# Expert stage of a fused attention, gated-layer and expert kernel: additions, scatters and gathers moved to later steps of the next unit

## The chip, the core and the metric

The kernel runs on one core of one Trainium2 chip. A time is microseconds on the device for one execution. Engines are named as the profile names them: PE (TensorE, matrix multiplication; PEld its weight loads), DVE (VectorE), ACT (ScalarE), POOL (GpSimd), SP (SyncE, which issues most DMAs). Each engine works through its own list of instructions in order. An instruction that waits holds up everything behind it on its engine. The clock of TensorE is granted by a throttle, and the profile shows the granted share.

## The reference

Three layers follow one another; the change lies in the last.

```python
def reference(**kwargs):
    attn_out = _attn_ref(**attn_kwargs)                 # queries pooled by 2, 16 heads of 64
    x = attn_out ... reshape(B * S, H * D)              # 1152 tokens of 512
    x = _moe_ref(x=x, **moe_kwargs)                     # rms norm, silu(x @ w_gate) * (x @ w_val) @ w_out
    return _moe2_ref(x=x, **moe2_kwargs)

def _moe2_ref(x, w_gate, w_noise, noise, w1, w2):
    ...                                                 # noisy logits of 8 experts, two best per token
    out = np.zeros((N, D), dtype=np.float32)
    for e in range(E):
        for k in range(2):
            mask = top2[:, k] == e
            if not mask.any():
                continue
            h = np.maximum(x[mask] @ w1[e], 0.0)        # 512 -> 1024
            out[mask] += top2_w[mask, k, None] * (h @ w2[e])   # 1024 -> 512
    return out.astype(np.float32)
```

All data are float32. A product on PE is made of three passes over operands that are split into a rounded part and a remainder ("hi" and "lo").

## The kernel before, in words

The tokens of an expert are put into blocks of 128. The expert stage, from about 537 us to the end, works through 14 **units** (`SEQ`, with two units ahead of it that the first half of the router chose). A unit is a **pair** (two blocks of one expert) or a **single** (one block). In the kernel before the units are pair, pair, pair, single, pair, single, pair, single, pair, single, pair, single, pair, pair, numbered 0 to 13. A further set of units stands in a branch that is taken only when there are more blocks; it isn't taken with these inputs.

Each unit has eight **steps** (0 to 7), one per piece of 512 KB of that expert's weights (`W[u, i]`, split into hi by ACT, L106, and lo by DVE, L1005, five steps ahead by `wsplit`). Steps 0 to 3 are the first layer (`up_pair` L1072 or `up_one` L1087). In a pair each step ends with `up_evac`: ACT makes the rounded hidden part (L1076), DVE the remainder (L1077). The PSUM tile `ph` has two buffers, so step 2 waits for the evacuation of step 0, and step 3 for that of step 1. In a single the hidden rows are evacuated by ACT and turned on PE by `h_trans`, half 0 after step 2 and half 1 after step 4. Steps 4 to 7 are the second layer (`down`, L1099), which adds up into a PSUM tile `py` for each block.

Around them run, in program order:

- `finish(u)`: for each block DVE computes `yo = py * weight + pr` (L1131; L1129 in unit 0, which adds nothing), and POOL issues the scatter of the rows to the output (L1132). The next scatter waits for the one before to land, because both write the output. Before, the call for unit u stands after step 0 of unit u + 1.
- `gather_o(u)`: POOL issues the gather of the output rows that unit u will add to (tile `pr`, L1027), one per block. It waits until the scatters of unit u - 1 have landed. Before, it stands after step 2 of unit u.
- `gather_x(u + 2)` (tile `xg`, L1021) after step 5 of unit u: input rows for the unit after the next, also on POOL; its buffer comes free when `x_trans(u + 1)` and `weight(u + 1)` (DVE, `wv`), at the same step, have read it.
- `x_trans` and `h_trans` go through `tsplit`: four transposes on PE, the rounded part by ACT (L975), the remainder by DVE (L977). They share two PSUM banks in turn (`bank()`), so in a single the four calls h 0, h 1, x block 0, x block 1 alternate between the banks. The transposes of x block 1 wait until DVE has evacuated h 1.

The last unit, 13, is followed by its own `finish`, block 0 and then block 1, after all its `down` steps, which alternate between the blocks.

Unit 0 is written out by hand at the end of the program, interleaved with the second half of the router. There `run(gB)` issues the rest of `r_assign`: positions of the tokens (`pp`), sums on POOL (`sm`, `mx`, L747 and L749), a count per expert on PE (`pn`, L754), and a row of small DVE operations. The PSUM pool of units 1 to 13 (`pm`, opened by `open_psum`) lies over the banks of the earlier pool. Its tiles get their places in the order in which their names are first used: before, `ph` first and then `py`.

Of the kernel before, what the change touches and what calls it, by code (L numbers as in the profile page):

```python
# [9 lines left out]
F32 = mybir.dt.float32  # L10
# [11 lines left out]
def fused_kernel(ctx, tc, q, k, v, w_gate, w_val, w_out, rms_g,  # L22
                 r_gate, r_noise, noise, e_w1, e_w2, out, dbg=None):
    nc = tc.nc
    P = 128
# [482 lines left out]
    DM = H * D  # L508
# [132 lines left out]
    def bank_(spec, nm):  # L641
        pl, tg, nb = spec
        return pl.tile([P, 512], F32, name=nm, tag=tg, bufs=nb)
# [79 lines left out]
    def r_assign(t0, nt):  # L723
        ts_ = slice(t0, t0 + nt)
        M, mmb = R["M"], R["mmb"]
        idx = R["idx"][:, ts_]
        n = nt * NE
        pp = bank_((ps, "gv1", 2) if t0 else BANK[0], "pp")[:, 0:n].rearrange("p (t e) -> p t e", t=nt)
        for t in range(t0):
            pe.matmul(pp, R["onesb"], mmb[:, t, None, :].to_broadcast([P, nt, NE]), start=(t == 0), stop=False)  # L730
        dve.tensor_copy(idx, R["x8"][:, ts_, 0:2])
        yield
        dve.tensor_tensor(M[:, ts_], R["i8"][:, None, None, :].to_broadcast([P, nt, 2, NE]),
                          idx[:, :, :, None].to_broadcast([P, nt, 2, NE]), op=ALU.is_equal)
        yield
        dve.tensor_tensor(mmb[:, ts_], M[:, ts_, 0], M[:, ts_, 1], op=ALU.add)
        yield 1
        pe.matmul(pp, R["lt"], mmb[:, ts_], start=(t0 == 0), stop=False)
        for t in range(nt - 1):
            pe.matmul(pp[:, t + 1:], R["onesb"], mmb[:, t0 + t, None, :].to_broadcast([P, nt - 1 - t, NE]),  # L740
                      start=False, stop=(t == nt - 2))
        P_ = R["S"][:, 0, ts_]
        mx, sm = rtile(f"mx{t0}", [P, NE, NT], BF16), rtile(f"sm{t0}", [P, nt, NE], BF16)
        with nc.allow_low_precision("integers up to 5"):
            a = mmb[:, t0]
            for t in range(1, nt - 1):
                pool.tensor_tensor(sm[:, t], a, mmb[:, t0 + t], op=ALU.add)  # L747
                a = sm[:, t]
            pool.tensor_tensor(mx, a[:, :, None].to_broadcast([P, NE, NT]),  # L749
                               mmb[:, t0 + nt - 1, :, None].to_broadcast([P, NE, NT]), op=ALU.add)  # L750
        if t0:
            PB["n"] = bank_((ps, "gv1", 2), "pn")
            for m in ("mx0", f"mx{t0}"):
                pe.matmul(PB["n"][0:NCOL, 0:2], R[m].rearrange("p e j -> p (e j)"), R["onesb"][:, 0:2],  # L754
                          start=(m == "mx0"), stop=(m != "mx0"))
        dve.tensor_tensor(P_, pp, R["base8"][:, None, :].to_broadcast([P, nt, NE]), op=ALU.add)
        yield
        dve.tensor_tensor(M[:, ts_], M[:, ts_], P_[:, :, None, :].to_broadcast([P, nt, 2, NE]), op=ALU.mult)
        yield
        aki, cs = R["aki"][:, :, ts_], R["cs"][:, :, ts_]  # L760
        with nc.allow_low_precision("integers below 2 ** 24"):
            dve.tensor_reduce(aki[:, 0], M[:, ts_], axis=AX.X, op=ALU.add)
        yield
        dve.tensor_scalar(aki[:, 1], aki[:, 0], 7, None, op0=ALU.logical_shift_right)
        yield
        dve.tensor_scalar(aki[:, 2], aki[:, 0], 127, None, op0=ALU.bitwise_and)
        yield
        dve.tensor_copy(cs, aki[:, 1:3])
        yield
# [147 lines left out]
    def r_index(pl):  # L917
# [12 lines left out]
    RAW = []  # L930
    REG = {}
    SEQ = [None, None] + [(True, 0), (False, 0), (True, 1), (False, 1), (True, 2), (False, 2), (True, 3), (False, 3),
                          (True, 4), (False, 4), (True, 5), (True, 6)]
    NU1 = len(SEQ)
    SEQ += [(True, r) for r in range(NPS, NPA)] + [(False, r) for r in range(NSS, NSA)]

    def nblk(u):
        return 2 if u < 2 or SEQ[u][0] else 1
# [48 lines left out]
    def experts():  # L987
        mo = ctx.enter_context(tc.tile_pool(name="mo", bufs=1, reuse_waits="tile"))
# [35 lines left out]
        def gather_o(u):  # L1024
            PR[u] = wps[0].tile([P, 2, DM], F32, name="pr", tag="ws21", bufs=1)
            for k in range(nblk(u)):
                pool.indirect_dma_start(out=PR[u][:, k], out_offset=None, in_=out,  # L1027
                                        in_offset=bass.IndirectOffsetOnAxis(ap=col(u, k, "gidx"), axis=0))
# [61 lines left out]
                act.activation(HS[u, h], PL[u, h], AF.Relu)  # L1090

        def down(u, i, k):
            if i == 4:
                PL[u, "y", k] = pbank("py")
            w, x = W[u, i], HTT[u]
            f0 = 2 * (i - 4)
            for z, (a, c) in enumerate(PASS):
                for d in range(2):
                    pe.matmul(PL[u, "y", k], x[c][:, f0 + d, k * P:k * P + P], w[a][:, d],  # L1099
                              start=i == 4 and z + d == 0, stop=i == 7 and z == 2 and d == 1)  # L1100

        def piece(u, i):
            if i >= 4:
                for k in range(nblk(u)):
                    down(u, i, k)
            elif nblk(u) == 2:
                up_pair(u, i, 0)
                up_pair(u, i, 1)
                up_evac(u, i)
            else:  # L1110
                up_one(u, i)
# [8 lines left out]
                                         op0=ALU.is_equal, op1=ALU.mult)  # L1120
            dve.tensor_tensor(wv[:, 2, 0:n], wv[:, 0, 0:n], wv[:, 1, 0:n], op=ALU.add)

        def finish(u):
            n = nblk(u)
            yo = YO[u] = mo.tile([P, 2, DM], F32, name="yo", tag="yo", bufs=1)
            for k in range(n):
                w = WV[u][:, 2, k:k + 1]
                if u == 0:
                    dve.tensor_scalar(yo[:, k], PL[u, "y", k], w, 1.0, op0=ALU.mult, op1=ALU.mult)  # L1129
                else:  # L1130
                    dve.scalar_tensor_tensor(yo[:, k], PL[u, "y", k], w, PR[u][:, k], op0=ALU.mult, op1=ALU.add)  # L1131
                pool.indirect_dma_start(out=out, out_offset=bass.IndirectOffsetOnAxis(ap=col(u, k, "sidx"), axis=0),  # L1132
                                        in_=yo[:, k], in_offset=None, bounds_check=B * SQ - 1, oob_is_err=False)
# [7 lines left out]
        def units(u0, u1, skip=0):  # L1141
            todo = [(u, i) for u in range(u0, u1) for i in range(8)]
            if not skip:
                gather_x(u0)
                gather_o(u0)
                for i in range(8):
                    wload(u0, i)
                for a in todo[:LEAD]:
                    wsplit(*a)
                x_trans(u0)  # L1150
                weight(u0)
                if u0 + 1 < u1:
                    gather_x(u0 + 1)
                    for i in range(8):
                        wload(u0 + 1, i)
                for u, i in todo[:LEAD]:
                    if u + 2 < u1:
                        wload(u + 2, i)
            for n_, (u, i) in enumerate(todo):
                if n_ < skip:  # L1160
                    continue
                piece(u, i)
                if nblk(u) == 1:
                    if i == 2:
                        h_trans(u, 0)
                    if i == 4:
                        h_trans(u, 1)
                if i == 0 and u > max(u0, 1):
                    finish(u - 1)
                if i == 2 and u > max(u0, 1):  # L1170
                    gather_o(u)
                if i == 5 and u + 1 < u1:
                    x_trans(u + 1)
                    weight(u + 1)
                    if u + 2 < u1:
                        gather_x(u + 2)
                if n_ + LEAD < len(todo):
                    v_, j = todo[n_ + LEAD]
                    wsplit(v_, j)
                    if v_ + 2 < u1:  # L1180
                        wload(v_ + 2, j)
            finish(u1 - 1)

        def open_psum():
            pm.append(ctx.enter_context(tc.tile_pool(name="pm", bufs=1, space=PSUM, reuse_waits="tile")))

        def rest():
            open_psum()
            units(0, NU1, 8)
            more = nc.values_load(R["more"][0:1, 0:1], min_val=0, max_val=1)  # L1190
            with tc.If(more > 0):
                units(NU1, len(SEQ))
# [53 lines left out]
    for f in range(2, NFP - 2):  # L1246
        u0 = 32 * f
# [17 lines left out]
    def run(g, n=1000):  # L1265
        if n < 1000 and skip.get(id(g), 0):
            skip[id(g)] -= 1
            return
        for z in itertools.islice(g, n):
            if z and n < 1000:  # L1270
                skip[id(g)] = z - 1
                return
# [111 lines left out]
    run(gB, 1)  # L1384
    up_evac(0, 3)
    down(0, 4, 0)
    run(gB)
    w_hi(0, 7)
    down(0, 4, 1)
    run(gW)  # L1390
    run(gC, 2)
    x_trans(1)
# [61 lines left out]
```

## Time and profile before

| | |
|---|---|
| median of 3 runs | 847.99 us (843.16 to 853.68) |
| profiled execution | 845.21 us, span of its instructions 843.3 us |
| busy in the span | PE 791.6 us, DVE 580.2 us, ACT 421.4 us, POOL 299.7 us |
| mean granted clock of PE | 0.979 |

A row of a timeline reads: start in us, duration, engine, line, operation, destination and sources, shape, and in brackets how long the engine sat idle before it and what released it. A row of waits reads: engine and line that waited, for whom, us in total, how many times, and the longest.

### The profile page before, as it was taken

How to read it: one execution, taken by the hardware profiler on the slowest of the kernel's cores; microseconds unless marked ns; L12 is line 12 of the kernel's file. 1: busy time of each engine (PE TensorE's matmuls, PEld its weight loads, DVE VectorE, ACT ScalarE, POOL GpSimd, SP SyncE). 2: the span in 40 equal slices, each digit the busy share in tenths (PEclk: the TensorE clock that was granted, in tenths of full speed). 3: DMA queues.
4: the chain of work that ended last, by engine and by line, in shares of the span. 5: the costliest groups of instructions: out<-in, count | busy, mean ns of one | idle time of the engine just before them, and what ended most of it. 6: DMA issues, size and time to landing. Idle time of an engine off the chain costs nothing.

```text
span 843.3 us, 14036 instructions
## 1 busy us (share of the span) xinstructions
PE 791.6 (94%) x5282; PEld 681.8 (81%) x5282; DVE 580.2 (69%) x838; ACT 421.4 (50%) x823; POOL 299.7 (36%) x251
## 2 busy tenths in 40 slices
PE   5999999999897989999999999989998999999993
PEld 4777777767675779999999999879987988888992
DVE  6668668677678866766787646686684876777750
ACT  4655655656565644442333252554464646456530
POOL 8747647649233521311132100112232432323410
PEclk9999999999999989999999999999999999999997
DMA  7344222221132211422141016639997888888210
GB/s 208 87 135 146 66 90 71 73 69 30 43 115 72 80 51 51 147 78 76 54 147 54 1 52 230 204 127 367 320 308 249 283 273 290 254 277 293 98 47 21
DMA packets 72940, 118.83 MB, mean 141 GB/s; under 512 B 7583, under 2 KB 37279, under 8 KB 72865
## 3 DMA queue, kind: packets, MB, share of 16 engines
q1 hardware_dynamic: 67504, 101.55, 38.0%
q0 software_dynamic: 5360, 16.31, 5.6%
q8 instruction: 43, 0.70, 0.4%
q14 instruction: 33, 0.26, 0.1%
HBM read 103.66 MB, written 10.77 MB: 136 GB/s over the span
## 4 chain that ended last, share of the span: by engine, by line
PE 67%; DVE 12%; issue 7%; DMA 4%; ACT 4%; POOL 4%; POOLq 0%; DVEq 0%; ACTq 0%
PE gv L528 14%; PE py L1099 11%; PE ph L1072 8%; PE po L549 8%; PE av L229 7%; PE st L202 4%; PE s L188 3%; DMA pr<-out_dram,gidx 3%; PE st L203 3%; PE ph L1087 3%; PE tt L135 2%; DVE wz L1005 2%; DVE Ql L193 1%; PE xt L972 1%; DVE es L217 1%
## 5 line engine op out<-in xcount | busy, mean ns | idle before, releaser
L528 PE MATMUL gv<-XN,ws 128*128 128x256 f32 (+1 forms) x1152 | 168.2, 299 | 4.1 <-ACT sl L536 3.7
L528 PEld LDWEIGHTS gv<-XN,ws 128*128 128x128 f32 x1152 | 159.8, 191 | 10.1 <-ACT sl L536 3.9
L1005 DVE TENSOR_TENSOR wz<-raw,wz 128x1024 fp32r<-128x1024 f32 x112 | 133.9, 1221 | 16.5 <-ACT wz L106 16.2
L193 DVE TENSOR_REDUCE Ql<-s 128x1 fp32r<-128x1152 f32 x72 | 97.3, 1354 | 57.5 <-PE s L188 43.5
L1099 PE MATMUL py<-wz,hTT 128*128 128x512 f32 x552 | 134.2, 395 | 0.0
L204 ACT ACTIVATE et<-st 128x288 f32<-128x288 f32 x288 | 103.0, 413 | 52.5 <-PE st L203 48.2
L106 ACT CAST wz<-raw 128x1024 fp32r<-128x1024 f32 x112 | 113.4, 1046 | 8.0 <-PE py L1099 8.0
L1099 PEld LDWEIGHTS py<-wz,hTT 128*128 128x128 f32 x552 | 100.7, 188 | 20.3 <-DVE hTT L977 0.9
L1072 PE MATMUL ph<-xgT,wz 128*128 128x256 f32 x768 | 95.3, 285 | 9.0 <-DVE hTT L1077 7.7
L1072 PEld LDWEIGHTS ph<-xgT,wz 128*128 128x128 f32 x768 | 94.1, 191 | 10.8 <-DVE hTT L1077 8.4
L398 POOL TENSOR_TENSOR ws<-wm,ws 128x1024 fp32r<-128x1024 f32 x18 | 43.3, 2407 | 151.1 <-ACT ws L397 97.0
L202 PE MATMUL st<-QH,KT 128*128 128x288 f32 x288 | 91.1, 331 | 5.5 <-ACT et L204 4.0
L549 PE MATMUL po<-ws,hT 128*128 128x512 f32 x324 | 84.5, 400 | 0.1
L203 PE MATMUL st<-QlT,KT 128*128 128x288 f32 x288 | 81.9, 298 | 0.0
L229 PE MATMUL av<-et,v 128*64 128x288 f32 x576 | 81.5, 419 | 0.0
L202 PEld LDWEIGHTS st<-QH,KT 128*128 128x128 f32 x288 | 55.0, 191 | 20.4 <-ACT et L204 11.7
L549 PEld LDWEIGHTS po<-ws,hT 128*128 128x128 f32 x324 | 59.5, 192 | 11.1 <-ACT hT L538 0.5
L217 POOL TENSOR_TENSOR accp<-accp,et 128x576 f32<-128x576 f32 x32 | 48.2, 1507 | 55.7 <-ACT et L204 35.1
L1132 POOL DMA_INDIRECT out_dram<-yo,sidx x23 | 29.2, 1271 | 103.2 <-DVE yo L1131 51.3
L538 ACT CAST hT<-sl 128x256 fp32r<-128x256 f32 (+1 forms) x48 | 20.8, 433 | 88.8 <-DVE sl L537 88.8
L229 PEld LDWEIGHTS av<-et,v 128*64 128x64 f32 x576 | 37.6, 138 | 26.0 <-issue 5.9
L1076 ACT ACTIVATE hTT<-ph 128x512 fp32r<-128x512 f32 x36 | 21.6, 599 | 70.3 <-PE ph L1072 70.3
(250 smaller groups left out, 1172.8 us busy)
## 6 DMA issues: line engine op xcount, KB each, us to landing
raw<-in_moe_w_dram SPq DMA_DIRECT2D x112, 512.0 KB, 5.7
wraw<-in_moe_w_gate_dram SPq DMA_DIRECT2D x6, 1024.0 KB, 5.1
wraw<-in_moe_w_val_dram SPq DMA_DIRECT2D x6, 1024.0 KB, 7.9
wraw<-in_moe_w_out_dram SPq DMA_DIRECT2D x6, 1024.0 KB, 5.3
kraw<-in_k_dram SPq DMA_DIRECT2D x16, 288.0 KB, 4.1
v<-in_v_dram SPq DMA_DIRECT2D x8, 576.0 KB, 3.7
KT<-KT SPq DMA_DIRECT2D x16, 288.0 KB, 3.2
Qraw<-in_q_dram SPq DMA_DIRECT2D x16, 256.0 KB, 4.5
```

The costliest lines, as they stand in the source:

```text
L106: act.copy(o, i)
L193: dve.tensor_reduce(Ql[p % 3][h][:, c, D:D + 1], t[:, :, 0:384], axis=AX.XY, op=ALU.max, negate=True)
L202: pe.matmul(t[:, 0:NG], KT[p, h][:, cs], QhT[p, h][:, n0:n0 + NG], start=True, stop=False)
L203: pe.matmul(t[:, 0:NG], KT2[h][p % NKT[h]][:, cs], QlT[p, h][:, n0:n0 + NG], start=False, stop=True)
L204: act.activation(et[:, h, :], t[:, 0:NG], AF.Exp, scale=SCALE)
L217: eng.tensor_tensor(acc, acc, e, op=ALU.add)
L229: pe.matmul(av[h * D:(h + 1) * D, 0:NG], V[p][:, h, c, :], ET[p, g, c][:, h, :], start=(c == 0), stop=(c == KC - 1))
L528: pe.matmul(t[:, 0:n], w[a][:, d, j * P:(j + 1) * P], XN[hf][b_][:, d, cs], start=(k_ == 0), stop=(k_ == 11))
L549: pe.matmul(pt, HT[f, hf][a][:, j, c0:c0 + P], w[b_][:, j, :], start=(k_ == 0), stop=(k_ == 5))
L1005: eng.tensor_tensor(lo, RAW[u % 2][i], hi.bitcast(F32), op=ALU.subtract)
L1072: pe.matmul(o, w[a][:, d, j * P:j * P + P], XT[u][c][:, d], start=z + d == 0, stop=z == 2 and d == 3)
L1099: pe.matmul(PL[u, "y", k], x[c][:, f0 + d, k * P:k * P + P], w[a][:, d], start=i == 4 and z + d == 0, stop=i == 7 and z == 2 and d == 1)
```

## The change

Five edits. (1) `finish(u - 1)` is called after step 3 of unit u, no longer after step 0, and `gather_o(u)` after step 6, no longer after step 2, so behind `gather_x(u + 2)`. In the last unit both are called after step 1. (2) Units 11 and 12 change places: the order is now pair (10), pair (11), single (12), pair (13). (3) In the last unit the second layer is done block by block: the four `down` steps of block 0, its `finish`, then those of block 1. (4) `py` is the first tile that the PSUM pool gives out, so it lies on the banks where `ph` lay before, and `ph` on later banks. (5) The count per expert (`pn`) is issued one `down` later in unit 0.

```diff
         if t0:
+            yield
             PB["n"] = bank_((ps, "gv1", 2), "pn")
...
-                          (True, 4), (False, 4), (True, 5), (True, 6)]
+                          (True, 4), (True, 5), (False, 4), (True, 6)]
...
-            if i == 4:
+            if (u, "y", k) not in PL:
                 PL[u, "y", k] = pbank("py")
...
-        def finish(u):
-            n = nblk(u)
-            yo = YO[u] = mo.tile([P, 2, DM], F32, name="yo", tag="yo", bufs=1)
-            for k in range(n):
+        def finish(u, ks=None):
+            if u not in YO:
+                YO[u] = mo.tile([P, 2, DM], F32, name="yo", tag="yo", bufs=1)
+            yo = YO[u]
+            for k in range(nblk(u)) if ks is None else ks:
...
-                piece(u, i)
+                last = u == u1 - 1
+                if not last or i < 4:
+                    piece(u, i)
                 if nblk(u) == 1:
                     if i == 2:
                         h_trans(u, 0)
-                    if i == 4:
+                    if i == 4 - last:
                         h_trans(u, 1)
-                if i == 0 and u > max(u0, 1):
-                    finish(u - 1)
-                if i == 2 and u > max(u0, 1):
-                    gather_o(u)
+                if u > max(u0, 1):
+                    if i == (1 if last else 3):
+                        finish(u - 1)
+                    if i == (1 if last else 6):
+                        gather_o(u)
...
-            finish(u1 - 1)
+
+            u = u1 - 1
+            for k in range(nblk(u)):
+                for i in range(4, 8):
+                    down(u, i, k)
+                finish(u, [k])
...
             open_psum()
+            PL[1, "y", 0] = pbank("py")
             units(0, NU1, 8)
...
-    run(gB)
+    run(gB, 1)
     w_hi(0, 7)
     down(0, 4, 1)
+    run(gB)
```

On DVE, in unit 3 (a single), before. `hTT` are the remainders of the hidden rows, halves 0 and 1; `xgT` that of the next unit's input:

```order
569 L1131 SCALAR_TENSOR_TENSOR yo<-py,wv,pr 128x512 x2
570 L1005 TENSOR_TENSOR wz<-raw_5869,wz 128x1024
571 L1005 TENSOR_TENSOR wz<-raw_5870,wz 128x1024
572 L977 TENSOR_TENSOR hTT<-xt,hTT 128x4x128
573 L1005 TENSOR_TENSOR wz<-raw_5871,wz 128x1024
574 L1005 TENSOR_TENSOR wz<-raw_5581,wz 128x1024
575 L977 TENSOR_TENSOR hTT<-xt,hTT 128x4x128
576 L1005 TENSOR_TENSOR wz<-raw_5581,wz 128x1024
577 L977 TENSOR_TENSOR xgT<-xt,xgT 128x4x128 x2
```

and in the changed kernel:

```order
569 L1006 TENSOR_TENSOR wz<-raw_5869,wz 128x1024
570 L1006 TENSOR_TENSOR wz<-raw_5870,wz 128x1024
571 L978 TENSOR_TENSOR hTT<-xt,hTT 128x4x128
572 L1006 TENSOR_TENSOR wz<-raw_5871,wz 128x1024
573 L1133 SCALAR_TENSOR_TENSOR yo<-py,wv,pr 128x512 x2
574 L1006 TENSOR_TENSOR wz<-raw_5581,wz 128x1024
575 L978 TENSOR_TENSOR hTT<-xt,hTT 128x4x128
576 L1006 TENSOR_TENSOR wz<-raw_5581,wz 128x1024
577 L978 TENSOR_TENSOR xgT<-xt,xgT 128x4x128 x2
```

The two additions of the pair before (`yo`) now stand between the two halves of `hTT`.

On POOL, from the additions of unit 1 to the gather for unit 4 (`xg` input rows, `pr` output rows), before:

```order
164 L1132 DMA out_dram<-yo,sidx_5735 1152x512 x2
165 L1027 DMA pr<-out_dram,gidx 128x512 x2
166 L1021 DMA xg<-XD,gidx 128x516 x2
167 L1132 DMA out_dram<-yo,sidx 1152x512 x2
168 L1027 DMA pr<-out_dram,gidx 128x512
169 L1021 DMA xg<-XD,gidx 128x516
```

and in the changed kernel:

```order
164 L1134 DMA out_dram<-yo,sidx_5735 1152x512 x2
165 L1022 DMA xg<-XD,gidx 128x516 x2
166 L1028 DMA pr<-out_dram,gidx 128x512 x2
167 L1134 DMA out_dram<-yo,sidx 1152x512 x2
168 L1022 DMA xg<-XD,gidx 128x516
169 L1028 DMA pr<-out_dram,gidx 128x512
```

In every unit the gather of output rows now stands right behind the gather of input rows.

## Rows read from the trace of the kernel before

**Rows 1.** The page: busy time, share of the span and instructions of each engine.
```profile
PE 791.6 (94%) x5282; PEld 681.8 (81%) x5282; DVE 580.2 (69%) x838; ACT 421.4 (50%) x823; POOL 299.7 (36%) x251
```

**Rows 2.** Waits of PE from 520 us on: total us, times, longest.
```profile
PE ph L1072 <- DVE hTT L1077: 7.7, 3, 3.2
PE ph L1072 <- DVE yo L1129: 0.9, 1, 0.9
PE pn L754 <- POOL mx L749: 0.9, 1, 0.9
```

**Rows 3.** Timeline of units 7 and 8: additions, scatters, the gather, the stalled matmul.
```profile
694.29 1.02 POOL L1132 DMA_INDIRECT out_dram<-yo,sidx  x1 [0.30 <-issue]
...
701.66 1.56 POOL L1132 DMA_INDIRECT out_dram<-yo,sidx  x1 [6.35 <-DVE wz L1005]
...
707.20 1.77 POOL L1027 DMA_INDIRECT pr<-out_dram,gidx  x1 [3.97 <-DVE wz L1005]
...
715.34 0.75 DVE L1131 SCALAR_TENSOR_TENSOR yo<-py,wv,pr 128x512 f32<-128x512 f32 x1 [4.71 <-DMA pr<-out_dram,gidx]
...
717.88 3.08 PE L1072 MATMUL ph<-xgT,wz 128*128 128x256 f32 x24 [2.91 <-DVE hTT L1077]
```

**Rows 4.** Stretches behind unit 4's stall: busy by engine, then PEclk, DMA, GB/s.
```profile
640.00:642.00 2.00, 0.97 (x6) 0.98 (x7) 2.00 (x3) 0.00 (x0) 1.27 (x1) 0.87 0.56 20
642.00:644.00 2.00, 2.00 (x11) 2.00 (x11) 1.83 (x3) 0.00 (x0) 0.00 (x0) 0.50 0.65 247
644.00:646.00 2.00, 2.00 (x14) 1.91 (x13) 0.00 (x0) 0.32 (x1) 0.51 (x1) 0.78 1.06 346
```

**Rows 5.** Timeline of unit 7, a single: its additions, its first matmuls, and DVE later.
```profile
693.09 1.40 DVE L1131 SCALAR_TENSOR_TENSOR yo<-py,wv,pr 128x512 f32<-128x512 f32 x2
...
693.26 4.39 PE L1087 MATMUL ph<-wz,xgT 128*128 128x256 f32 x36
...
699.69 1.23 DVE L1005 TENSOR_TENSOR wz<-raw,wz 128x1024 fp32r<-128x1024 f32 x1
...
701.13 1.23 DVE L1005 TENSOR_TENSOR wz<-raw,wz 128x1024 fp32r<-128x1024 f32 x1 [0.21 <-ACT wz L106]
...
702.27 0.68 DVE L977 TENSOR_TENSOR hTT<-xt,hTT 128x512 fp32r<-128x512 f32 x1
...
702.57 1.09 PE L972 MATMUL xt<-ident,xg 128*128 128x128 f32 x8
```

**Rows 6.** Timeline of POOL: unit 1's scatters, later the input gathers issued in unit 6.
```profile
598.65 1.01 POOL L1132 DMA_INDIRECT out_dram<-yo,sidx  x1 [6.70 <-DVE yo L1131]
605.04 0.99 POOL L1132 DMA_INDIRECT out_dram<-yo,sidx  x1 [5.38 <-DVE wz L1005]
...
690.32 1.40 POOL L1021 DMA_INDIRECT xg<-XD,gidx  x1 [4.64 <-PE py L1099]
692.02 1.97 POOL L1021 DMA_INDIRECT xg<-XD,gidx  x1 [0.30 <-issue]
```

**Rows 7.** Instructions by tile: time to landing of the gathers to `pr`, then `xg`.
```profile
DMA to landing us min/median/max: 4.1/5.2/6.2
...
DMA to landing us min/median/max: 6.1/7.6/8.8
```

**Rows 8.** Timeline of the last unit, 13, and the end.
```profile
811.42 1.02 POOL L1132 DMA_INDIRECT out_dram<-yo,sidx  x1 [16.21 <-DVE yo L1131]
...
815.01 1.00 POOL L1132 DMA_INDIRECT out_dram<-yo,sidx  x1 [2.56 <-DVE wz L1005]
...
817.60 11.09 PE L1099 MATMUL py<-wz,hTT 128*128 128x512 f32 x48
...
828.39 1.02 POOL L1132 DMA_INDIRECT out_dram<-yo,sidx  x1 [8.10 <-DVE yo L1131]
828.73 0.75 DVE L1131 SCALAR_TENSOR_TENSOR yo<-py,wv,pr 128x512 f32<-128x512 f32 x1 [0.61 <-PE py L1099]
...
832.61 1.00 POOL L1132 DMA_INDIRECT out_dram<-yo,sidx  x1 [3.19 <-DMA out_dram<-yo,sidx]
```

## The prediction, made before the changed kernel was run

> **What bounds the kernel now.** I read the engines' totals first. PE is busy for 791.6 us of 843.3 [rows 1], so an edit gains only where it takes idle time from PE, shortens the tail behind its last matmul, or spares PE a low clock.
>
> The waits of PE come next, from the start of the expert stage. Three waits of first-layer matmuls for DVE's `hTT` sum to 7.7 us, the longest 3.2. One for the additions of unit 0 takes 0.9, and one of the count `pn` for POOL's sums 0.9 [rows 2].
>
> The timeline tells where the three come from. Unit 6's two scatters start 7.4 us apart (694.29, 701.66), as the second waits for the first. The gather for unit 7 follows 5.5 later (707.20), and its addition starts 8.1 after that (715.34). DVE stood 4.71 us in front of that addition. Behind it was the `hTT` on which step 3 of unit 8 waits, so PE stood 2.91 us [rows 3]. A single is too short for two scatters and a gather in a row (21 us). Behind unit 4's stall, the one of 3.2 us, the granted clock falls to 0.87, 0.50 and 0.78 in three stretches of 2 us (0.50 is the level of 1.2 GHz of the two) [rows 4]. That is (0.13 + 0.50 + 0.22) x 2 = 1.7 us of lost work.
>
> Last, the end: the last matmul ends at 817.60 + 11.09 = 828.7, the last scatter is issued at 832.61, held by the one before it [rows 8].
>
> **The start, edits 4 and 5: a gain of 1.8 us.** With `ph` on later banks, unit 1's first matmul no longer waits for unit 0's additions: 0.9. With six `down` matmuls ahead of `pn`, POOL's sums run under them: 0.9. DVE's work on the router starts with the next transposes, which move up with PE, so I count both in full [rows 2]. Lower bound 0.9, if DVE's chain to unit 1 absorbs one of them.
>
> **The stalls removed, edit 1: a gain of 7.7 us, and 1.7 of clock.** In a pair the addition now stands behind all four `hTT` of the unit. PE then has a second layer of 11.1 us (48 matmuls [rows 8]) whose weights were split earlier. If the gather is 2 us late there, DVE loses those 2 us under it. So the waits [rows 2] and the low clock [rows 4] go.
>
> **The cost in singles: 6.0 us.** There the addition is put where DVE has no room. In unit 7 (first matmul at 693.26) DVE ends a split at 699.69 + 1.23 = 700.92, 7.66 us in, and waits 0.21 before the next (701.13). Then it makes `hTT` of half 1 until 702.95, and the transposes of x block 1 use the same bank right behind it (their row lasts 1.09 us from 702.57) [rows 5]. Two additions take 1.40 (693.09) and stood, until now, at the start of the single, where DVE had time. Now they come between these splits: 1.40 - 0.21 = 1.2 us that PE waits, in each of five singles (3, 5, 7, 9 and 12). Less only if DVE's order leaves slack that I don't see.
>
> **The gather behind the input gather: 4.8 us.** In a pair `gather_o` now follows `gather_x` on POOL. The input gathers of unit 6 start at 690.32, 2.94 before unit 7, and the second is issued until 693.99, 0.7 into it [rows 5, 6]. The row gathers follow from 1.0 in, 1.0 each and 0.30 between, so their issues end at 2.0 and 3.3. With the median landing of 5.2 [rows 7] they land at 7.2 and 8.5. The first is in time for 7.66, the second addition ends at 9.25 and not at 7.66 + 1.40 = 9.06: 0.2 late. That is the low end.
>
> A transfer behind input gathers is slower, though. The scatter at 694.29, right behind the gather of 692.02, let the next go after 7.4 us, the one at 598.65, with none just ahead, after 6.4 [rows 3, 6]. With that 1.0 the second addition ends at 10.25, 1.2 late. Were the landing that of the input gathers (7.6 [rows 7]), it would be 2.6 late: the high end. I take 0.7, between the first two, as the median is from the same operation but mostly from gathers with nothing ahead. Units 5, 7 and 9: 2.1 (0.6 to 7.8).
>
> The Trainium skill (DMA: Bandwidth & Descriptors, section SWDGE vs HWDGE vs iDMA) speaks against the change here: DMAs that POOL issues get one queue only, and each engine drains its ring packet by packet, so a later gather stands behind an earlier one. The 7.4 against 6.4 us agrees with it. By that rule the lateness would be 1.2 in every one of the four singles, 2.0 us more in all.
>
> Unit 3 is worse, because unit 2 follows a pair: both scatters of unit 1 now start behind step 3 of unit 2. Counted from unit 3's start, that addition stands at about -9.9 (second layer 11.1, transposes 0.4, the last evacuation 1.6 into it). The first scatter is at -8.9, the second 6.4 later at -2.5, and landed 5.5 later at 3.0 [rows 3, 6]. So the row gathers start at 3.0 and not 1.0: 2.0 on top, 2.7 late (2.2 to 4.6). Unit 12 comes when the weights are loaded. A scatter lets the next go after 3.6 there [rows 8], and gathers land in about the 4.1 of the shortest [rows 7]: not late (0 to 1.0).
>
> Unit 3's stall is then 1.2 + 2.7 = 3.9 us, longer than the one with the low clock, so I charge 1.7 for the clock again (0, or 3.4 for two such).
>
> **The end, edit 3: a gain of 2.8 us.** Block 0 is done half of 11.1 us before PE's end, at 823.2. Its scatter follows at 824.2 and lets another go 4.2 later (as 828.39 to 832.61 [rows 8]), at 828.4. Block 1's addition starts at 828.73 as before and its scatter at 829.8, not 832.61. The row gather must be there: the additions of unit 12 come some 7.2 us into unit 13, then scatter 1.0 + 4.2, gather 1.0 + 4.1, so 17.5, against 16.9 for block 0's last matmul. The rest is hidden by block 1's 5.5 us. If the gather were 5 us later, the gain would be gone.
>
> **Edit 2** changes no unit's work. It puts a single before the last unit, so one scatter precedes the last gather and not two. Costed at nothing, by the sum just made.
>
> **Sum.** Gains 1.8 + 7.7 + 1.7 + 2.8 = 14.0, costs 6.0 + 4.8 + 1.7 = 12.5: 1.5 us less than the profiled execution's 845.21, or 843.7; forecast **844 us**, no change that can be measured. The shown median, 847.99, is 0.3% above that execution. By the terms' ends this forecast reaches from 840 (costs 8.8) to 847 (costs of 15 to 16). By the skill's rule alone the sum would be 845.7.
>
> **Rivals.**
>
> *The additions hide everywhere* (chance 0.22). If PE doesn't wait for half 1 in singles, because ACT's order and not DVE's sets it, only unit 3's 2.2 us remain: 845.2 - 14.0 + 2.2 = 833. For it: DVE is busy for 580 of 843 us [rows 1] and gathers land in 5.2 at the median. Against: the 0.21 us of room in the row.
>
> *The row gather becomes the wait* (0.21), ending slower. Place: half 1 in singles 3, 5, 7 and 9, behind an addition whose gather is queued behind two input gathers. Price at the landing of the input gathers, 7.6: lateness 2.6 x 3 + 4.6 + 1.0 = 13.4, with 6.0, and two stalls with a low clock, 3.4: 22.8 against 14.0, or 854. It decides from 0.4 us more per single than I took: 4 x 0.4 makes up the 1.5 of the sum. For it: the order on POOL and the 7.4. Against: the longest landing of a row gather so far is 6.2 [rows 7].
>
> *The middle stays as it is* (0.05): the stalls in pairs move behind step 3 with their size, since DVE there also makes the next unit's `xgT`, and only start and end gain: 4.6, or 840.6.
>
> The forecast has 0.52. The range of 8 in 10 runs from 834 to 854: rivals of both sides at their worked-out times, and runs of the kernel before differ by 1.2% among themselves. A change of 2% (about what a measurement can tell here) is beyond all of these: it needs 831 or 865. Even the whole 14.0 us is 1.7%. Faster by more 0.05, within 0.91, slower by more 0.04.
>
> **What would show it.** After the change the waits of PE should have no `ph` behind L1129 and no `pn` behind `mx`. First-layer matmuls of pairs should not wait for `hTT`. PE should idle instead in front of the second x transposes of each single, 1.2 us or more, most in unit 3, with DVE's additions behind gathers there. The last scatter should start about 1.1 us behind the last matmul. I am wrong if PE runs through the singles (then 833), or if the gathers to `pr` land after 7 us or more there (then 850 and up).

## The result, and the profile after

| | before | changed |
|---|---|---|
| median of 16 runs | 850.80 us (843.16 to 854.49) | 841.87 us (838.41 to 845.55) |
| profiled execution | 845.21 us, span 843.3 | 845.55 us, span 843.3 |
| ratio of the times | | 0.9895, 95% interval 0.9873 to 0.9918 |

The changed kernel is 1.05% faster, 8.9 us. That is less than 2%, so no change by the bound of the prediction, and 841.87 lies in its range. But the interval excludes 1, and the forecast put the change at 1.5 us. The two profiled executions hide the gain: that of before lies near the lower end of its runs, that of the changed kernel is the longest of its own. Their spans are equal.

The page's totals of the changed kernel, which answer to [rows 1]:

```profile
PE 794.3 (94%) x5282; PEld 683.7 (81%) x5282; DVE 581.2 (69%) x838; ACT 422.0 (50%) x823; POOL 303.6 (36%) x251
```

The numbers of instructions are the same, and no engine's busy time differs by as much as 4 us. The waits of PE from 520 us on, as in [rows 2], begin in the changed kernel with this one:

```profile
PE xt L973 <- DVE hTT L978: 10.5, 5, 3.6
```

The three rows of [rows 2] are gone: no first-layer matmul waits for `hTT` or for `yo`, and no wait of `pn` is listed. One new row takes their place, five waits in front of x transposes, one for each single. Unit 5 shows how one arises (timeline of the changed kernel; POOL's gathers first, then DVE and PE):

```profile
650.87 1.44 POOL L1022 DMA_INDIRECT xg<-XD,gidx  x1 [1.84 <-PE py L1100]
652.62 1.94 POOL L1022 DMA_INDIRECT xg<-XD,gidx  x1 [0.30 <-issue]
654.86 0.95 POOL L1028 DMA_INDIRECT pr<-out_dram,gidx  x1 [0.30 <-issue]
656.11 0.94 POOL L1028 DMA_INDIRECT pr<-out_dram,gidx  x1 [0.30 <-issue]
...
658.91 1.23 DVE L1006 TENSOR_TENSOR wz<-raw,wz 128x1024 fp32r<-128x1024 f32 x1
...
662.35 0.75 DVE L1133 SCALAR_TENSOR_TENSOR yo<-py,wv,pr 128x512 f32<-128x512 f32 x1 [2.21 <-DMA pr<-out_dram,gidx]
...
663.45 0.75 DVE L1133 SCALAR_TENSOR_TENSOR yo<-py,wv,pr 128x512 f32<-128x512 f32 x1 [0.35 <-DMA pr<-out_dram,gidx]
664.12 1.22 DVE L1006 TENSOR_TENSOR wz<-raw,wz 128x1024 fp32r<-128x1024 f32 x1
...
665.25 0.68 DVE L978 TENSOR_TENSOR hTT<-xt,hTT 128x512 fp32r<-128x512 f32 x1
...
665.99 0.69 PE L973 MATMUL xt<-ident,xg 128*128 128x128 f32 x4 [3.59 <-DVE hTT L978]
```

The gathers to `pr` are issued right behind the input gathers. DVE is done with its split at 660.14 and stands 2.21 us for the first gather. The two additions, a split and the `hTT` of half 1 follow, and PE, which has only the x transposes next, stands 3.59 us. In unit 12, at the end of the weight loads, nothing is late, and PE still stands:

```profile
802.23 1.40 DVE L1133 SCALAR_TENSOR_TENSOR yo<-py,wv,pr 128x512 f32<-128x512 f32 x2
...
804.68 0.69 DVE L978 TENSOR_TENSOR hTT<-xt,hTT 128x512 fp32r<-128x512 f32 x1
...
805.43 0.66 PE L973 MATMUL xt<-ident,xg 128*128 128x128 f32 x4 [0.85 <-DVE hTT L978]
```

So I take 0.85 us as the price of the additions' place alone, and what a single waits beyond it as the gather's lateness; an experiment below tests that. The other waits of this execution are 1.91 (unit 3), 1.69 (unit 7) and 2.46 (unit 9).

The clock (stretches of 20 us of the changed kernel; PE busy, PEclk, DMA share, GB/s):

```profile
650.00:670.00 20.00, 16.41 (x97) 0.91 0.93 313
670.00:690.00 20.00, 20.00 (x138) 1.00 0.80 262
...
730.00:750.00 20.00, 17.55 (x109) 0.91 0.90 298
```

The clock falls behind two of the five waits, those of 3.59 and 2.46. Each costs 0.09 x 20 = 1.8 us, about the 1.7 that [rows 4] gave.

The end, as in [rows 8]:

```profile
820.20 11.09 PE L1100 MATMUL py<-wz,hTT 128*128 128x512 f32 x48
...
825.88 0.75 DVE L1133 SCALAR_TENSOR_TENSOR yo<-py,wv,pr 128x512 f32<-128x512 f32 x1 [4.16 <-PE py L1100]
826.91 1.02 POOL L1134 DMA_INDIRECT out_dram<-yo,sidx  x1 [4.47 <-DVE yo L1133]
...
832.35 1.00 POOL L1134 DMA_INDIRECT out_dram<-yo,sidx  x1 [4.42 <-DVE yo L1133]
```

The last scatter starts 832.35 - 831.29 = 1.06 us behind the last matmul, as against 832.61 - 828.69 = 3.9 before. It waits for its addition, no longer for the scatter ahead of it. In a second execution it starts 1.43 us behind (828.61 - 827.18).

### The profile page after: what moved, and what is told of

Read it like the earlier page. It is cut to its first block, busy times and chain, and to the rows that moved or that the text cites. A ratio compares the mean times of both kernels' runs of the same rounds, so it can differ in the third digit from the quotient of the medians.

```text
span 843.3 us, 14029 instructions
## 1 busy us (share of the span) xinstructions
PE 794.3 (94%) x5282; PEld 683.7 (81%) x5282; DVE 581.2 (69%) x838; ACT 422.0 (50%) x823; POOL 303.6 (36%) x251
## 5 line engine op out<-in xcount | busy, mean ns | idle before, releaser
L1100 PE MATMUL py<-wz,hTT 128*128 128x512 f32 x552 | 137.2, 401 | 0.0
L1100 PEld LDWEIGHTS py<-wz,hTT 128*128 128x128 f32 x552 | 102.9, 192 | 20.9 <-DVE hTT L978 0.7
L1073 PE MATMUL ph<-xgT,wz 128*128 128x256 f32 x768 | 92.8, 281 | 0.0
L1134 POOL DMA_INDIRECT out_dram<-yo,sidx x23 | 32.1, 1395 | 131.5 <-DVE yo L1133 96.0
L203 PEld LDWEIGHTS st<-QlT,KT 128*128 128x128 f32 x288 | 55.5, 193 | 0.0
```

The source lines that it names most:

```text
L203: pe.matmul(t[:, 0:NG], KT2[h][p % NKT[h]][:, cs], QlT[p, h][:, n0:n0 + NG], start=False, stop=True)
L1073: pe.matmul(o, w[a][:, d, j * P:j * P + P], XT[u][c][:, d], start=z + d == 0, stop=z == 2 and d == 3)
```

## The experiments

In the sums below a ratio is turned into time with 850.8 us. Each ratio is to runs of the kernel before that were made beside that kernel's.

### How much does the kernel before wait in another execution?

The unchanged kernel before, profiled again, with these expectations:

> The kernel before, unchanged, for a second trace and more times. Theory 1 (the profiled execution of before was typical): first-layer matmuls wait about 7.7 us for hTT in three stalls, one low clock after them, span about 843. Theory 2 (that execution was a quick one, the middle of 16 runs being 850.8): span 847 to 852, with hTT waits of 10 to 14 us and two or three stretches of low clock behind them.

Measured: 851.52 us, ratio 1.000 (0.9972 to 1.0029). The profiled execution took 851.85. Its wait of first-layer matmuls for `hTT`, and the four stalled matmuls:

```profile
PE ph L1072 <- DVE hTT L1077: 12.4, 4, 3.8
...
638.85 4.49 PE L1072 MATMUL ph<-xgT,wz 128*128 128x256 f32 x24 [3.03 <-DVE hTT L1077]
679.37 4.62 PE L1072 MATMUL ph<-xgT,wz 128*128 128x256 f32 x24 [3.12 <-DVE hTT L1077]
719.38 4.60 PE L1072 MATMUL ph<-xgT,wz 128*128 128x256 f32 x24 [2.46 <-DVE hTT L1077]
760.80 4.63 PE L1072 MATMUL ph<-xgT,wz 128*128 128x256 f32 x24 [3.83 <-DVE hTT L1077]
```

And its stretches with a lower clock (PE busy, PEclk, DMA share, GB/s):

```profile
630.00:650.00 20.00, 16.97 (x107) 0.91 0.75 243
...
670.00:690.00 20.00, 16.88 (x107) 0.91 0.75 236
...
710.00:730.00 20.00, 17.55 (x112) 0.91 0.79 250
...
750.00:770.00 20.00, 16.17 (x104) 0.91 0.72 228
```

The same program has here four stalls, 12.4 us in all, and four clock stretches of 1.8. The execution that the prediction rests on had 7.7 us in three [rows 2] and, from 550 us on, one such stretch [rows 4]. What the change removes is thus up to 12.4 + 7.2 = 19.6 us and not 7.7 + 1.7 = 9.4.

### One part of the change alone

Edits 4 and 5 alone (the start):

```diff
         if t0:
+            yield
...
+            PL[1, "y", 0] = pbank("py")
...
-    run(gB)
+    run(gB, 1)
...
+    run(gB)
```

> Kernel before with edits 4 and 5 alone (PSUM places, count one step later). My terms: 0.9 + 0.9 us, so 1.8 us faster (ratio 0.998); waits of PE for L1129's additions and for POOL's mx gone, the hTT stalls unchanged. Rival: everything from unit 1 on only shifts, and the DVE chain of the router takes back one of the two: 0.9 us or nothing.

Measured: 847.68 us, ratio 0.9977 (0.9947 to 1.0006): 2.0 us. The waits for `yo` and `mx` are gone from its trace and those for `hTT` stay, so the edits act only where they should:

```profile
PE ph L1073 <- DVE hTT L1078: 11.0, 4, 3.4
```

The interval alone just includes no change.

Edit 3 alone (the last unit's second layer by blocks; additions and gathers stay where they were):

```diff
-                piece(u, i)
+                last = u == u1 - 1
+                if not last or i < 4:
+                    piece(u, i)
...
-            finish(u1 - 1)
+            u = u1 - 1
+            for k in range(nblk(u)):
+                for i in range(4, 8):
+                    down(u, i, k)
+                finish(u, [k])
```

> Kernel before with edit 3 alone (last unit's second layer block by block; order of units and places of additions and gathers as before). My term: 2.8 us faster (ratio 0.997), last scatter issued about 1.1 us after the last matmul and not 3.9. Rival: the first scatter isn't landed by then, or the row gather is late, and 0 to 1 us is left.

Measured: 847.33 us, ratio 0.9961 (0.9938 to 0.9984): 3.3 us, where the prediction had 2.8. In its trace the last scatter starts 837.63 - 836.28 = 1.35 us behind the last matmul. The middle, which this edit leaves alone, has four stalls again:

```profile
PE ph L1072 <- DVE hTT L1077: 12.0, 4, 3.4
```

Edit 1 alone (additions and gathers moved):

```diff
-                if i == 0 and u > max(u0, 1):
-                    finish(u - 1)
-                if i == 2 and u > max(u0, 1):
-                    gather_o(u)
+                if u > max(u0, 1):
+                    if i == (1 if last else 3):
+                        finish(u - 1)
+                    if i == (1 if last else 6):
+                        gather_o(u)
```

> Kernel before with edit 1 alone (additions after step 3, gathers after step 6, both after step 1 in the last unit; order of units as before). My terms: stalls of 7.7 and clock 1.7 removed, 10 to 12 us of waits in singles with one or two low clocks added: 0 to 2 us either way. If the usual execution of before has larger stalls and more low clocks than the profiled one (theory 2), 3 to 6 us faster (ratio 0.993 to 0.996).

Measured: 848.76 us, ratio 0.9977 (0.9952 to 1.0002): 2.0 us faster, or nothing. By the prediction's terms edit 1 alone was a loss: 12.5 - 9.4 = 3.1 us. Its trace, of its shortest run, has the new waits and none of first-layer matmuls for `hTT`:

```profile
PE xt L972 <- DVE hTT L977: 10.2, 5, 2.4
```

The five are 1.80 to 2.38 us long, and no stretch of 20 us from 550 to 810 us has a lower clock.

### The changed kernel again, and the order of units undone

The unchanged changed kernel, profiled again:

> The changed kernel, unchanged, for a second trace and more times beside the kernels of this call. Five stalls in singles of 9 to 11 us in all, one or two stretches of low clock; ratio to before 0.988 to 0.991. If the equal spans of the two first traces were the rule and not chance: ratio 0.997 or more.

Measured: 842.03 us, ratio 0.9898 (0.9863 to 0.9934), span 839.6. The waits of x transposes for `hTT` sum to 8.8 us in five (1.85, 2.04, 1.90, 2.18, 0.84), two clock stretches again. So two executions bracket the new cost at 8.8 to 10.5, with 3.6 of clock.

Edit 2 undone, the rest of the change kept:

```diff
-                          (True, 4), (True, 5), (False, 4), (True, 6)]
+                          (True, 4), (False, 4), (True, 5), (True, 6)]
```

> Changed kernel with units 11 and 12 back in the old order (edit 2 undone). My term for edit 2 was nothing by itself, but block 0 of the last unit then waits for two scatters: last gather some 4 us later, tail gain of 2.8 partly gone: 0 to 2 us slower than the changed kernel, ratio to before 0.989 to 0.992.

Measured: 844.41 us, ratio 0.9921 (0.9895 to 0.9947), so edit 2 gives 2.2 us (0.0026), though the intervals overlap. The trace shows two places where it can come from. The waits in singles, and the end, in that kernel:

```profile
PE xt L973 <- DVE hTT L978: 11.0, 5, 2.9
...
817.32 11.09 PE L1100 MATMUL py<-wz,hTT 128*128 128x512 f32 x48
817.61 1.00 POOL L1134 DMA_INDIRECT out_dram<-yo,sidx  x1 [2.56 <-DVE wz L1006]
821.12 0.99 POOL L1028 DMA_INDIRECT pr<-out_dram,gidx  x1 [2.51 <-DMA out_dram<-yo,sidx]
822.41 0.97 POOL L1028 DMA_INDIRECT pr<-out_dram,gidx  x1 [0.30 <-issue]
...
827.15 1.02 POOL L1134 DMA_INDIRECT out_dram<-yo,sidx  x1 [3.77 <-DMA pr<-out_dram,gidx]
...
830.81 1.00 POOL L1134 DMA_INDIRECT out_dram<-yo,sidx  x1 [2.64 <-DMA out_dram<-yo,sidx]
```

With a pair ahead of the last unit, two scatters precede its gathers. Block 0's scatter waits for the second gather (827.15), holds block 1's, and the last scatter starts 830.81 - 828.41 = 2.4 us behind the last matmul, 1.3 later than the 1.06 above. The rest lies in the last single: it is unit 11 here, weights are still being loaded, and it waits 2.50 us where unit 12 waits 0.85.

### Is it the place of the additions, or the gathers?

The changed kernel without the gathers of output rows, so that units 1 to 13 scatter their products and add nothing:

```diff
-                if u == 0:
+                if True:
                     dve.tensor_scalar(yo[:, k], PL[u, "y", k], w, 1.0, op0=ALU.mult, op1=ALU.mult)
...
-                    if i == (1 if last else 6):
-                        gather_o(u)
```

> Changed kernel without the gathers of output rows: units 1 to 13 scatter py * weight and add nothing, so the parts of a token in different units aren't summed. Theory hold plus lateness: of the 10.5 us in singles the wait of each addition for its gather goes, the order on DVE stays, so five stalls of 0.85 us (that of unit 12, whose gather was in time), 4.3 in all, no low clock, and 6 to 10 us less than the changed kernel (ratio to before 0.978 to 0.983). Rival, DVE's order alone makes the stalls: they stay near 2 us each and the time near 0.989.

Measured: 831.31 us, ratio 0.9772 (0.9737 to 0.9806). Its wait for `hTT` and the first of the five stalls:

```profile
PE xt L973 <- DVE hTT L978: 4.3, 5, 0.9
...
622.54 0.66 PE L973 MATMUL xt<-ident,xg 128*128 128x128 f32 x4 [0.85 <-DVE hTT L978]
```

All five are 0.85 us, to the hundredth (DVE's two operations take 1.41 us there, the two additions 1.40), and no stretch from 550 to 810 us has a lower clock. The gain on the changed kernel, 842.03 - 831.31 = 10.7 us, is a little over the 6 to 10 expected. The place costs 5 x 0.85 = 4.3 us. The gathers cost the rest, 10.5 - 4.3 = 6.2 in the first execution and 8.8 - 4.3 = 4.5 in the second, and the clock with it.

The additions in singles behind step 4, so behind the `hTT` of half 1, the gathers as in the changed kernel:

```diff
-                    if i == (1 if last else 3):
+                    if i == (1 if last else 3 if nblk(u) == 2 else 4):
                         finish(u - 1)
```

> Changed kernel with the additions in singles one place later, behind hTT of half 1 (the end of step 4). Theory 1 (the place on DVE costs): the stall before the second x transposes goes, 5 to 10 us less than the changed kernel, ratio to before 0.978 to 0.984. Theory 2 (the loop of scatter, scatter, gather, addition, scatter, gather, 38 to 40 us against 36 of PE work for a pair and a single, sets the pace): two us later into the loop, so the wait comes back elsewhere, in pairs at xgT or for input rows, ratio 0.985 to 0.992.

Measured: **832.41 us, ratio 0.9779 (0.9749 to 0.9809)**, faster than both kernels: 9.5 us under the changed one. Its timeline in unit 5:

```profile
658.75 0.68 DVE L978 TENSOR_TENSOR hTT<-xt,hTT 128x512 fp32r<-128x512 f32 x1
...
659.06 1.08 PE L973 MATMUL xt<-ident,xg 128*128 128x128 f32 x8
...
660.12 0.75 DVE L1133 SCALAR_TENSOR_TENSOR yo<-py,wv,pr 128x512 f32<-128x512 f32 x1 [0.69 <-DMA pr<-out_dram,gidx]
...
661.13 0.75 DVE L1133 SCALAR_TENSOR_TENSOR yo<-py,wv,pr 128x512 f32<-128x512 f32 x1 [0.27 <-DMA pr<-out_dram,gidx]
...
664.27 5.90 PE L1073 MATMUL ph<-xgT,wz 128*128 128x256 f32 x48 [0.91 <-DVE xgT L978]
```

DVE still waits for the gathers, and from 560 us on for 21.8 us in ten waits, where the changed kernel had 11.4 in nine. But PE has its eight transposes and the rest of the second layer meanwhile. Only 1.4 us reaches it, in two waits for `xgT`, and no stretch from 550 to 810 us has a lower clock. The second theory, in which the loop of scatters and gathers sets the pace, had 0.985 to 0.992 and is excluded. A late gather costs nothing where the instruction that waits for it stands behind what PE needs.

### Is the lateness the order of the gathers on POOL?

The changed kernel with the gather of output rows at step 5 and so ahead of the input gather:

```diff
-                    if i == (1 if last else 6):
+                    if i == (1 if last else 5):
                         gather_o(u)
```

> The changed kernel with the gather of the output rows one step earlier, behind step 5, so that it stands ahead of the gather of the input rows on POOL and not behind it. Theory (the lateness behind the additions in singles is the queueing of the row gather behind two input gathers): in the changed kernel's trace the row gathers of unit 4 start at 654.86 and 656.11, the input gathers at 650.87 and 652.62; ahead of them they would start about 2 to 3.5 us earlier, in time for the additions, and the waits of x transposes for hTT would fall from 8.8 to 10.5 us to about the 0.85 per single that the kernel without row gathers showed, 4.3 us in five; with the low clock behind unit 5 and unit 9 gone as well, 842.0 - 5 - 2 = about 835 to 837 us. Rival (the scatter before the gather is what ends last, or the input gathers, now behind a wait for that scatter, become late): the row gather waits for the scatter's landing, 4 us or more, the input gathers start 3 to 5 us later, and x transposes wait for xg instead: 841 to 846 us.

Measured: 835.40 us, ratio 0.9816 (0.9764 to 0.9868). Its waits of PE, two of the five stalls, and POOL in unit 4:

```profile
PE xt L973 <- DVE hTT L978: 4.7, 5, 1.3
PE xt L973 <- DMA xg<-XD,gidx: 0.8, 2, 0.4
...
624.76 0.66 PE L973 MATMUL xt<-ident,xg 128*128 128x128 f32 x4 [1.29 <-DVE hTT L978]
...
662.22 0.66 PE L973 MATMUL xt<-ident,xg 128*128 128x128 f32 x4 [0.85 <-DVE hTT L978]
```

```profile
648.48 1.46 POOL L1028 DMA_INDIRECT pr<-out_dram,gidx  x1 [3.82 <-DMA out_dram<-yo,sidx]
650.24 1.94 POOL L1028 DMA_INDIRECT pr<-out_dram,gidx  x1 [0.30 <-issue]
652.48 1.84 POOL L1022 DMA_INDIRECT xg<-XD,gidx  x1 [0.30 <-issue]
654.62 0.95 POOL L1022 DMA_INDIRECT xg<-XD,gidx  x1 [0.30 <-issue]
```

The waits fall to the 0.85 of the place (0.85 to 0.87) in every single but unit 3, and the clock stays full from 550 to 810 us. The rival is answered too: the row gather does wait 3.82 us for the scatter, and the input gathers do stand behind it, but that costs PE 0.4 us. (Of the two waits for `xg`, the one of 0.33 us at 530.10 lies ahead of unit 1.)

The same edit in the kernel with the additions behind half 1:

> The same earlier row gather, in the kernel whose additions stand behind half 1 of the hidden rows in singles (832.4 us, 0.978 of the kernel before). Theory: PE no longer waits for a row gather there (its waits for xgT sum to 1.4 us), so an earlier gather gives at most 1 us: 831.5 to 833 us. Rival (the late gathers still cost through DVE's order): 829 to 831. If the input gathers become late, waits for xg appear and it is slower, 834 to 838.

Measured: 834.95 us, ratio 0.9826 (0.9775 to 0.9877). Its interval overlaps with that of the kernel without the edit (0.9749 to 0.9809), so no gain is shown. The trace has 2.2 us of waits for `xg`; that kernel has 0.3, and those ahead of unit 1. So the third of the three expectations, late input gathers, is the one that the runs point to. Once the additions are out of the way, an earlier row gather has nothing left to save.

## Why the prediction was right, and where it was not

Each edit's terms against what its own experiment gave (minus is faster, us):

| part | predicted | measured | by its interval |
|---|---|---|---|
| start, edits 4 and 5 | -1.8 | -2.0 | -4.5 to +0.5 |
| end, edit 3 | -2.8 | -3.3 | -5.3 to -1.4 |
| middle, edit 1 (12.5 - 9.4) | +3.1 | -2.0 | -4.1 to +0.2 |
| order of units, edit 2 | 0 | -2.2 | two intervals that overlap |
| sum | -1.5 | -9.5 | |
| all together | | -8.9 | -10.8 to -7.0 |

Each part is known to 2 or 3 us only, so it is partly luck that 9.5 comes so near to 8.9.

**The mechanism held.** The waits that should go went, the new wait stands where it was put (second x transposes of each single, behind `hTT`), and the last scatter starts 1.06 and 1.43 us behind the last matmul in two executions, as against 1.1 forecast. The new wait sums to 10.5 and 8.8 us in two executions, with 6.0 + 4.8 = 10.8 forecast. The first rival, where PE runs through the singles, and the third, where the stalls move with their size, are excluded by that row. The second, the row gather as the wait, is true as a mechanism, but at 4.5 to 6.2 us and not at 13.4.

**The step that was mis-sized is "The stalls removed, edit 1: a gain of 7.7 us, and 1.7 of clock".** It read both from one execution, the 845.21 us one, 5.6 us under the median of 16 runs. A second execution, 851.85 us, had 12.4 and 7.2. The first was the odd one: the two kernels that leave the middle alone have four stalls too. The table follows the part from the first matmul of unit 1 to the end of the last matmul, in nine executions. Low clock is what the clock cost, read in stretches of 2 us, so a little under the 1.8 each of the longer stretches; all in us.

| execution | this part | waits for DVE | low clock | the rest |
|---|---|---|---|---|
| kernel before, the one predicted from | 258.8 | 7.7 | 1.7 | 249.4 |
| kernel before, second | 267.6 | 12.4 | 6.9 | 248.3 |
| start alone (middle as before) | 264.6 | 11.0 | 5.2 | 248.4 |
| end alone (middle as before) | 266.9 | 12.0 | 6.9 | 248.0 |
| edit 1 alone | 259.2 | 10.2 | 0 | 249.0 |
| changed, order of units undone | 263.0 | 11.0 | 3.4 | 248.6 |
| changed | 262.8 | 10.5 | 3.4 | 248.9 |
| changed, second | 261.2 | 8.8 | 3.4 | 249.0 |
| changed, additions behind half 1 | 249.9 | 1.4 | 0 | 248.5 |

The rest is the same within 1.4 us, so these waits and the clock are all that differs there. Three of the four executions with the old middle lose 16.2 to 19.3 us in it; the prediction read the fourth, 9.4. With edit 1 and the old order of units it is 10.2 (the shortest run of edit 1 alone) and 14.4. Against those three edit 1 is a gain, of 1.8 to 9.1 us; against the fourth it is a loss, of 0.8 to 5.0, where the prediction had 3.1. The runs of edit 1 alone showed a gain of 2.0. So the sign is accounted for; for the size these executions are too few.

**Why 844 was still near 841.87.** Two errors offset each other. The base was 5.6 us too low, and the sum of the change 7.4 too small. The prediction had the sign of it before it: it noted a shown median 0.3% above the profiled execution, and priced nothing by that. Two smaller slips stand in its bounds: the costs at the terms' high ends sum to 22.8, as its second rival has them, which gives 854 and not 847; and the 833 of its first rival lies outside the range that is said to hold both rivals.

**The price of the place was 0.85 and not 1.2 per single.** 1.40 - 0.85 = 0.55 us of room, where the 0.21 of one row [rows 5] was taken as all of it. The same rows hold a part of the rest: `hTT` of half 1 ended at 702.95, and the transposes that need its bank are the second four of a row of eight that started at 702.57 and lasts 1.09, so at about 703.1: another 0.17. That is argued and not tested, and what the last 0.17 is, no row says.

**The lateness was right in sum, wrong in place.** Forecast 2.7 in unit 3 and 0.7 in units 5, 7 and 9 (sum 4.8); measured 1.1, 2.7, 0.8 and 1.6 (sum 6.2, each wait less 0.85). Unit 3 was charged for two scatters 6.4 us apart. They came 3.6 apart there (605.69 and 609.31). The DMA engines moved 184 to 247 GB/s in the stretches of 2 us between them, and 274 to 377 in those between the two that were 6.4 apart. Unit 5 instead got its gathers 6.5 us after the issue ended (655.81 to 662.35), with two input gathers just ahead.

The cause, the row gather's place behind the input gathers, is shown by exchanging them: the wait falls to 0.85. The exchange does two things, though. The gather starts sooner, 8.7 us ahead of unit 5's `hTT` of half 0 (648.48 to 657.18), where the two executions of the changed kernel had 3.4 and 4.7. And its median landing is 5.4 us, where they had 5.8 and 7.5. How much of the lateness is the turn on POOL and how much the queue of transfers is not separated. The Trainium skill (DMA: Bandwidth & Descriptors, section SWDGE vs HWDGE vs iDMA) says that DMAs issued by POOL share one queue, drained packet by packet. The 5.4 against 7.5 agrees with it, the 5.4 against 5.8 hardly tells. By that rule the prediction had 2.0 us more, a lateness of 6.8; the 6.2 and 4.5 measured lie on both sides of the 4.8 taken, and don't decide.

**One sign was badly chosen.** "Gathers to `pr` land after 7 us or more, then 850 and up": the median landing was 5.8 us in the first execution and 7.5 in the second, and the second waited less (8.8 us against 10.5). A landing is counted per gather, while the wait depends also on when POOL got to issue it.

**Edit 2 was not free.** The sum for the last gather (17.5 against 16.9, the rest hidden) was made for one scatter ahead of it, but edit 2 was costed at nothing and not at what two scatters would cost: by the traces 1.0 to 1.3 us at the end and up to 1.6 in the last single, by the runs 2.2 in all.

## What to carry to other kernels

A stall that ends on a DMA or on the clock differs from one execution to the next: price its removal from several traces (here three of four showed about twice what the first did), or at least ask where the profiled execution lies among the runs. On an engine that works in order, put an operation that waits for a DMA behind the evacuation that TensorE needs next; here that one line gave 9.5 us on top of the 8.9 of the whole change. Where two gathers share a queue, issue first the one that is needed first, unless its reader can wait for free.

## What the runs showed of the hardware

Which stall brings the lower clock isn't told by its length. In the first execution of the kernel before it fell behind one of 3.2 us [rows 4] and not behind the one of 2.91 at 717.88 [rows 3]. In the second execution of the changed kernel it fell behind stalls of 2.04 and 2.18 us and not behind 1.85 and 1.90. With the order of units undone it fell behind 2.88 and 2.21 us and not behind 2.50, all three in one execution, and with edit 1 alone behind none of five stalls of up to 2.38. Just behind the longest stall of the changed kernel's first execution (3.59 us, up to 665.99) the granted clock, in stretches of 2 us with the busy times of PE, PEld, DVE, ACT and POOL ahead of it, was:

```profile
664.00:666.00 2.00, 0.01 (x1) 0.01 (x1) 2.00 (x4) 0.00 (x0) 1.72 (x1) 1.00 0.75 279
666.00:668.00 2.00, 2.00 (x8) 1.71 (x9) 2.00 (x3) 1.29 (x2) 0.23 (x1) 0.62 0.73 157
668.00:670.00 2.00, 2.00 (x6) 1.51 (x6) 1.97 (x6) 2.00 (x3) 0.00 (x0) 0.52 0.97 351
```

PE was idle at the full clock and lost it only once it worked again, so a sum of idle time misses what follows it, here (0.38 + 0.48) x 2 = 1.7 us.

A gather that goes second on POOL often lands later, but order is not all of it. Median landings of `pr` and `xg` were 5.2 and 7.6 us before [rows 7], where the input gathers went second; 7.5 and 4.6 in the second execution of the changed kernel, where the row gathers did; and 5.4 and 6.1 with the row gathers first again. In the first execution of the changed kernel they were equal, 5.8 and 5.9, and in the kernel without row gathers the input gathers took 7.5.
